# Last loads of a decode kernel reordered, value products placed by their landing, and a transposed FFN

## The chip, the cores and the metric

The kernel runs on one core of one Trainium2 chip. The metric is the device time of one execution in microseconds (us), the median of several runs. In the text, PE is TensorE (PEld its weight loads), DVE is VectorE, ACT is ScalarE, POOL is GpSimd and SP is SyncE, which here does nothing but issue transfers.

## What is computed

One decode step of a transformer layer in which attention and FFN work in parallel, for a batch of 4 with one token each:

```
xn = layernorm(x)                                  # x: 4 x 640
q  = xn @ wq                                       # 32 heads of 192
k, v = the last 2048 of 8192 cached positions      # per batch entry and head: 2048 x 192
o  = softmax(q k^T / sqrt(192)) v                  # per head
y  = x + o @ wo + (silu(xn @ w1) * (xn @ w3)) @ w2 # wo: 6144 x 640; w1, w3: 640 x 1536; w2: 1536 x 640
```

All inputs are bfloat16. The caches' windows are 32 key tiles and 32 value tiles of 3,072 KB; wq is 7,680 KB, wo is 7,680 KB, and w1, w3 and w2 are 1,920 KB each. Each byte is read once.

## The kernel before

**Tiles.** A head's keys are one tile `kt` of 128 partitions by 64 positions by 192: partition p holds 64 positions of one batch entry (32 partitions for each of the four entries). Its values are a tile `vt` of the same shape. There are two buffers for keys and three for values. The kernel writes its order by hand: `add(slot, phase, function, ...)` puts a step into a list, and the lists are run through by slot, and by phase within a slot. A slot u is a quarter of a head (16 positions); head h has the slots 4h to 4h+3, and 128 slots (`NU`) cover 32 heads. Every engine takes its instructions in that order.

**Scores.** `mult` (L202, DVE) multiplies a quarter of the key tile with the head's query, broadcast over the partitions. `adder` (L213, PE) adds six groups of 32 channels by six matmuls with the identity into a PSUM bank (two of these). `reduce_quarter` (L221, DVE) sums the 32 that are left. In slot u stand the product of u, the matmuls of u-1 and the reduction of u-2.

**Softmax.** For each head, over six slots: maximum in each partition (L225, DVE), transpose (L230, PE), maximum of each batch entry and its negative (L235, L238, DVE), broadcast back to the partitions (L243, PE), copy and exponential (L246, L249, ACT), and `chain_z` (L257, DVE), which spreads the exponentials over four columns, one for each batch entry. `ge_tot` (L278, PE) and `ge_norm` (L284, DVE) give the reciprocal of the sum.

**Values.** `pv` (L266, PE) is 32 matmuls for a head, each over two positions at once: 8 columns of z against 384 columns of V. The wanted results are two blocks of the product, the even position's in columns 0 to 191 and the odd position's in columns 192 to 383, on different partitions. `pv` comes in two halves of 16 matmuls, at slots 4h+10 and 4h+12 (`L` is 10). After the second, ACT copies the whole bank (128 x 384) to `o_raw` (L272). `ge_tr` (L294, PE) turns it and adds the blocks: six steps, each with one matmul for each of the two blocks, against the selection matrix `sel`; the profile counts 24 float32 matmuls for a head. `ge_copy` (L303, DVE) scales with the reciprocal into `oT`. For each group of four heads, `ge_proj` (`acc_add`, L194 and L195) multiplies with a tile of wo into two accumulators that live through the whole program; wo has two buffers.

**FFN.** w1, w3 and w2 share one buffer. `ffn_in` (L326) computes the gate and the up projection with xn as the weights: 15 matmuls of 512 columns for each matrix, copied by ACT; then SiLU (L331), the product (L337) and 12 transposes (L342). The product with w2 (24 matmuls of L194 and L195, behind everything else) ends the accumulation. L402 (DVE) and L403 (ACT) cast the accumulators, and L404 writes the output.

**Loads.** All transfers are issued by SP in program order, and SP waits where a buffer isn't free: x (L110), wq in three pieces (L116), the key tiles (L91, head h at slot 4(h-1)), the value tiles (L100, head h at slot 4h+2; head 29 at 4h+5; head 31 in two halves), wo (L106, group g at slot 16g+8, the last at slot 128), w1 and w3 (L318, slots 24 and 30), and w2 in three pieces (L350, slot 130). K31 is the key tile of head 31, V31 its value tile; wo6 and wo7 are the last two tiles of wo.

Of the kernel before, what the change touches and what calls it, by code (L numbers as in the profile page):

```python
# [10 lines left out]
FP32 = mybir.dt.float32  # L11
BF16 = mybir.dt.bfloat16
ALU = mybir.AluOpType
ACTF = mybir.ActivationFunctionType
AX = mybir.AxisListType
# [3 lines left out]
def kernel(  # L19
# [14 lines left out]
    KBUFS: int = 2,  # L34
    VBUFS: int = 3,
    PBUFS: int = 4,
    L: int = 10,
    FFN_HEAD: int = 6,
):
    nc = tc.nc  # L40
    P = 128
    B, Sq, D = A_x.shape
    _, H, Sk, Dh = A_k_cache.shape
    W = min(4096, max(256, Sk // 4))
    F = B_w1.shape[1]
    KC = D // P
    FC = F // P
    PB = P // B
    NJ = W // PB
    GQ = 4  # L50
# [4 lines left out]
    NG = H // HG  # L55
    CT = 32
    QW = HG * Dh
    RPP = QW // P
    NU = H * GQ
    N0 = D // 2  # L60
    N1 = D - N0
    QC = 512
# [1 line left out]
    assert D % P == 0 and F % QC == 0 and P % B == 0 and W % (PB * GQ) == 0  # L64
    assert JQ * DD == 512 and JQ % 2 == 0 and 2 * Dh <= 512 and 0 < N1 <= 512
    assert (H * Dh) % QC == 0 and NQ % 6 == 0 and QW % P == 0 and Dh % RPP == 0 and P == HG * CT
    assert 2 * H * Dh <= NJ * Dh and KBUFS == 2 and VBUFS == 3 and L == 10

    ctx.enter_context(tc.manual_schedule())
    const = ctx.enter_context(tc.tile_pool(name="const", bufs=1))  # L70
    fpool = ctx.enter_context(tc.tile_pool(name="ffn", bufs=1))
# [4 lines left out]
    small = ctx.enter_context(tc.tile_pool(name="small", bufs=3))  # L76
# [3 lines left out]
    ps_t = ctx.enter_context(tc.tile_pool(name="ps_t", bufs=1, space=MemoryType.PSUM))  # L80
# [3 lines left out]
    k_win = A_k_cache[:, :, Sk - W:Sk, :]  # L84
    v_win = A_v_cache[:, :, Sk - W:Sk, :]
    kts, vts, prs, pss, scs, exs, zs = {}, {}, {}, {}, {}, {}, {}
    wos, o_raws, rsums, rtbs, chs, ges, oTs = {}, {}, {}, {}, {}, {}, {}

    def load_k(h):
        kt = kpool.tile([P, NJ, Dh], BF16, tag="kt")  # L90
# [1 line left out]
                          in_=k_win[:, h].rearrange("b (p j) d -> p b (j d)", p=PB))  # L92
        kts[h] = kt

    def load_v(h, pieces=1):
        vt = vpool.tile([P, NJ, Dh], BF16, tag="vt")
        src = v_win[:, h].rearrange("b (p j) d -> p b j d", p=PB)
        n = NJ // pieces
        for i in range(pieces):
            nc.sync.dma_start(out=vt[:, i * n:(i + 1) * n, :].rearrange("q j d -> q (j d)"),  # L100
                              in_=src[:, :, i * n:(i + 1) * n, :].rearrange("p b j d -> p b (j d)"))
        vts[h] = vt

    def wo_load(hg):
# [2 lines left out]
        wos[hg] = wo_t  # L107

    x_sb = const.tile([B, D], BF16, name="x_sb")
    nc.sync.dma_start(out=x_sb[:], in_=A_x.rearrange("b s d -> (b s) d"))  # L110
    wq_v = A_wq.rearrange("(p kc) n -> p kc n", kc=KC)
    wq_rows = []
    for k0 in range(0, KC, 2):
        n = min(2, KC - k0)
        wt = vpool.tile([P, 2, H * Dh], BF16, tag="vt")
        nc.sync.dma_start(out=wt[:, 0:n, :].rearrange("p k n -> p (k n)"),  # L116
                          in_=wq_v[:, k0:k0 + n, :].rearrange("p k n -> p (k n)"))
        wq_rows += [wt[:, i, :] for i in range(n)]
    for h in range(KBUFS):
        load_k(h)  # L120

    idb = const.tile([P, P], BF16, name="idb")
    make_identity(nc, idb[:])
    idf = const.tile([P, P], FP32, name="idf")
# [6 lines left out]
    mask_b = const.tile([P, B], BF16, name="mask_b")  # L131
    nc.vector.tensor_copy(out=mask_b[:], in_=mask_f[:])

    sel = const.tile([P, 2 * B], FP32, name="sel")
    nc.vector.tensor_reduce(out=sel[:], in_=idf[:].rearrange("q (c k) -> q k c", k=CT)[:, 0:2 * B, :],
                            axis=AX.X, op=ALU.add)

    xf = ppool.tile([B, D], FP32, tag="pr")
    nc.vector.tensor_copy(out=xf[:], in_=x_sb[:])
# [22 lines left out]
    xnT = const.tile([P, KC, PB, B], BF16, name="xnT")  # L162
# [4 lines left out]
    for c0 in range(0, NQ, 6):  # L167
        qps = [pool.tile([P, QC], FP32, tag=tag, name="qps")
               for pool, tag in ((ps_add, "ps"), (ps_add, "ps"), (ps_o, "o_ps"), (ps_o, "o_ps"), (ps_m, "mt"), (ps_t, "t"))]
        for kc in range(KC):  # L170
            for i, qp in enumerate(qps):
                nc.tensor.matmul(qp[:], lhsT=xnT[:, kc].rearrange("p a b -> p (a b)"),  # L172
                                 rhs=wq_rows[kc][:, (c0 + i) * QC:(c0 + i + 1) * QC],
                                 start=(kc == 0), stop=(kc == KC - 1))
        for i, qp in enumerate(qps):
            dst = qbc[:, (c0 + i) * QC:(c0 + i + 1) * QC]
# [6 lines left out]
    o_banks = []  # L183
    for i in range(2):
        o_ps = ps_o.tile([P, 2 * Dh], FP32, tag="o_ps", name="o_ps")
# [7 lines left out]
    def acc_add(lhsT, rhs, first=False, last=False):  # L193
        nc.tensor.matmul(acc0[:], lhsT=lhsT, rhs=rhs[:, 0:N0], start=first, stop=last)  # L194
        nc.tensor.matmul(acc1[:], lhsT=lhsT, rhs=rhs[:, N0:D], start=first, stop=last)  # L195
# [62 lines left out]
                                in1=mask_b[:].unsqueeze(1).to_broadcast([P, NJ, B]), op=ALU.mult)  # L258
        zs[h] = z

    def pv(h, half):
        o_ps, z, vt = o_banks[h % 2], zs[h], vts[h]
        n = NJ // 4
        for jj in range(half * n, (half + 1) * n):
            c = jj % 4
            nc.tensor.matmul(o_ps[c * CT:c * CT + 2 * B, :], lhsT=z[:, 2 * jj:2 * jj + 2, :],  # L266
                             rhs=vt[:, 2 * jj:2 * jj + 2, :], start=(jj < 4), stop=(jj >= 2 * n - 4))
        if half == 1:
            zs.pop(h)
            vts.pop(h)  # L270
            o_raw = small.tile([P, 2, Dh], FP32, tag="o_raw", bufs=2, name="o_raw")
            nc.scalar.copy(out=o_raw[:].rearrange("q two d -> q (two d)"), in_=o_ps[:])  # L272
            o_raws[h] = o_raw


    def ge_tot(h):
# [10 lines left out]
    def ge_tr(h):  # L287
        hl = h % HG
        sl = slice(hl * CT, (hl + 1) * CT)
        gp = ps_t.tile([P, RPP, B], FP32, tag="t", name="gp")  # L290
        o_raw = o_raws.pop(h)
        for i in range(RPP):
            for part in range(2):
                nc.tensor.matmul(gp[sl, i, :], lhsT=o_raw[:, part, i:Dh:RPP], rhs=sel[:, part * B:(part + 1) * B],  # L294
                                 start=(part == 0), stop=(part == 1))
        ges[h] = gp

    def ge_copy(h):
# [9 lines left out]
        for i in range(i0, i1):  # L308
            acc_add(oT[:, i, :], wo_t[:, i * D:(i + 1) * D])

    h_sb = const.tile([B, F], BF16, name="h_sb")
    hT = const.tile([P, FC, B], BF16, name="hT")
    g_bf = const.tile([B, F], BF16, name="g_bf")
    ffn = {}

    def ffn_load(name, w):
# [1 line left out]
        nc.sync.dma_start(out=wt[:].rearrange("p k n -> p (k n)"), in_=w.rearrange("(p kc) n -> p (kc n)", kc=KC))  # L318
        ffn[name] = wt

    def ffn_in(name, dst):
        wt = ffn.pop(name)
        for n0 in range(0, F, QC):
            gt = ps_t.tile([B, QC], FP32, tag="t")
            for kc in range(KC):
                nc.tensor.matmul(gt[:], lhsT=xnT[:, kc, 0, :], rhs=wt[:, kc, n0:n0 + QC],  # L326
                                 start=(kc == 0), stop=(kc == KC - 1))
            nc.scalar.copy(out=dst[:, n0:n0 + QC], in_=gt[:])

    def ffn_silu():  # L330
        nc.scalar.activation(out=h_sb[:], in_=g_bf[:], func=ACTF.Silu)  # L331

    def ffn_up():
        ffn_in("w3", g_bf)

    def ffn_h():
        nc.vector.tensor_tensor(out=h_sb[:], in0=h_sb[:], in1=g_bf[:], op=ALU.mult)  # L337

    def ffn_transpose():
        hT_ps = ps_t.tile([P, FC, B], BF16, tag="t")  # L340
        for c in range(FC):
            nc.tensor.transpose(out=hT_ps[:, c, :], in_=h_sb[:, c:F:FC], identity=idb[0:B, 0:B])  # L342
        nc.vector.tensor_copy(out=hT[:], in_=hT_ps[:])

    w2_v = B_w2.rearrange("(p c) n -> p c n", c=FC)

    def w2_load(pieces):
        wt = fpool.tile([P, FC, D], BF16, tag="w", name="w2")
        for c0, c1 in pieces:
            nc.sync.dma_start(out=wt[:, c0:c1, :].rearrange("p c n -> p (c n)"),  # L350
                              in_=w2_v[:, c0:c1, :].rearrange("p c n -> p (c n)"))
        ffn["w2"] = wt

    sched = defaultdict(list)

    def add(slot, phase, fn, *args):
        sched[slot].append((phase, len(sched[slot]), fn, args))

    for h in range(H):
        u0, ul = h * GQ, h * GQ + GQ - 1  # L360
        if h >= KBUFS:
            add((h - KBUFS + 1) * GQ, 0, load_k, h)
        add(h * GQ + (2 if h != H - 3 else 5), 0, load_v, h, 1 if h < H - 1 else 2)
        for u in range(u0, ul + 1):
            add(u, 1, mult, u)
            add(u + 1, 2, adder, u)
            add(u + 2, 4, reduce_quarter, u)
        add(u0 + L, 3, pv, h, 0)
        add(u0 + L + 2, 3, pv, h, 1)
        add(ul + 2, 5, chain_lmax, h)  # L370
        add(ul + 3, 4, chain_tr, h)
        add(ul + 4, 5, chain_gmax, h)
        add(ul + 5, 4, chain_bc, h)
        add(ul + 6, 5, chain_z, h)
        add(ul + 6, 4, ge_tot, h)
        add(ul + 6, 6, ge_norm, h)
        add(u0 + L + 3, 3, ge_tr, h)
        add(u0 + L + 4, 5, ge_copy, h)
    for hg in range(NG):
        a = ((hg + 1) * HG - 1) * GQ + L + 5  # L380
        add(hg * HG * GQ + 8 if hg < NG - 1 else NU, 0, wo_load, hg)
        add(a, 3, ge_proj, hg, 0, RPP // 2)
        add(a + 1, 3, ge_proj, hg, RPP // 2, RPP)
    f = FFN_HEAD * GQ
    add(f, 0, ffn_load, "w1", B_w1)
    add(f + 5, 7, ffn_in, "w1", g_bf)
    add(f + 6, 7, ffn_silu)
    add(f + 6, 8, ffn_load, "w3", B_w3)
    add(f + 12, 7, ffn_up)
    add(f + 13, 7, ffn_h)  # L390
    add(f + 15, 7, ffn_transpose)
    add(NU + 2, 1, w2_load, [(0, FC // 2), (FC // 2, FC - 2), (FC - 2, FC)])

    for s in sorted(sched):
        for phase, _, fn, args in sorted(sched[s], key=lambda e: (e[0], e[1])):
            fn(*args)

    w2 = ffn.pop("w2")
    for c in range(FC):
        acc_add(hT[:, c, :], w2[:, c, :], last=(c == FC - 1))  # L400
    res = ppool.tile([B, D], BF16, tag="pr", name="res")
    nc.vector.tensor_copy(out=res[:, 0:N0], in_=acc0[:])  # L402
    nc.scalar.copy(out=res[:, N0:D], in_=acc1[:])  # L403
# [31 lines left out]
```

## Time and profile before

| What | Value |
|---|---|
| median of 5 runs | 534.62 us (532.68 to 535.16) |
| the profiled execution, time | 534.91 us |
| the profiled execution, span on the core | 533.1 us |
| mean clock granted to PE in it | 0.862 |
| PE busy | 380.3 us (71%) |
| DVE busy | 349.5 us (66%) |
| ACT busy | 48.1 us (9%) |
| read from HBM | 222.96 MB, 418 GB/s over the span |

The span is what the profiler's records cover on the core; the execution's time is 1.8 us longer. A group's row gives the source line, the engine, the operation with output and input, its shape and count, then busy time in all, mean ns of one, and the idle time of the engine just before these instructions with what ended most of it.

### The profile page before, as it was taken

What the parts mean: (1) busy time and instruction counts of PE and PEld (TensorE: products, weight loads), DVE (VectorE), ACT (ScalarE), POOL (GpSimd) and SP (SyncE); (2) the same over time, 40 slices, a digit from 0 to 9 for tenths busy, and PEclk for the clock granted to TensorE, in tenths of its full rate; (3) what the DMA queues carried; (4) which work ended last, traced back from release to release, by engine and by line L of the source; (5) the groups of instructions that cost most, each with busy time, mean ns of one, the idle gap of its engine ahead of it and who ended that gap; (6) DMA issues with size and microseconds to landing.
All of it is one profiled execution on the core that took longest, in us unless ns stands there. A gap on an engine that the chain in (4) does not pass through costs nothing.

```text
span 533.1 us, 6724 instructions
## 1 busy us (share of the span) xinstructions
PE 380.3 (71%) x2949; PEld 175.3 (33%) x2949; DVE 349.5 (66%) x471; ACT 48.1 (9%) x150; POOL 1.1 (0%) x8
## 2 busy tenths in 40 slices
PE   1876675759676686676848888566948777576987
PEld 0322232324232343233413334233413333232445
DVE  3178675867464776786756777587757776487861
ACT  2111100000222000000000000000000000000011
POOL 0000000000000000000000000000000000000000
PEclk9889877978789999597986779798897897798799
DMA  8999999999999999999999999999999999999993
GB/s 349 426 433 433 414 436 435 438 420 438 427 435 436 422 433 426 443 425 430 435 432 429 435 427 434 433 430 433 428 436 424 435 426 440 425 435 382 418 403 123
DMA packets 11709, 223.39 MB, mean 419 GB/s; under 512 B 1304, under 2 KB 1312, under 8 KB 2720
## 3 DMA queue, kind: packets, MB, share of 16 engines
q1 hardware_dynamic: 11680, 222.97, 97.8%
q8 instruction: 23, 0.38, 0.3%
q14 instruction: 6, 0.05, 0.0%
HBM read 222.96 MB, written 0.01 MB: 418 GB/s over the span
## 4 chain that ended last, share of the span: by engine, by line
DMA 59%; DVE 22%; PE 18%; issue 1%; ACT 0%; SPq 0%
DMA kt<-in_A_k_cache_dram 55%; DVE pr L202 16%; PE ps L213 8%; PE gp L294 5%; DVE sc L221 4%; DMA wt<-in_A_wq_dram 3%; PE qps L172 2%; PE o_ps L266 1%; PE acc L194 1%; PE acc L195 1%; DVE oT L303 0%; DVE rtb L284 0%; DVE qbc L178 0%; ACT o_raw L272 0%; DVE o_ps L186 0%
## 5 line engine op out<-in xcount | busy, mean ns | idle before, releaser
L213 PE MATMUL ps<-pr,idb 128*128 128x512 bf16 x768 | 222.7, 435 | 129.5 <-DVE sc L221 126.2
L202 DVE TENSOR_TENSOR pr<-kt,qbc 128x3072 bf16<-128x3072 bf16 x128 | 223.9, 1751 | 104.7 <-DMA kt<-in_A_k_cache_dram 103.6
L213 PEld LDWEIGHTS <-idb 128*128 128x128 bf16 x768 | 78.3, 106 | 226.1 <-issue 170.7
L221 DVE TENSOR_REDUCE sc<-ps 128x16 f32<-128x512 f32 x128 | 87.7, 685 | 8.2 <-PE ps L213 7.3
L266 PE MATMUL o_ps<-vt,z 128*8 128x384 bf16 x1024 | 58.1, 350 | 0.0
L294 PEld LDWEIGHTS gp<-sel,o_raw 128*32 128x32 f32 x768 | 46.8, 151 | 20.4 <-issue 18.7
L272 ACT COPY o_raw<-o_ps 128x384 f32<-128x384 f32 x32 | 15.3, 478 | 410.3 <-PE o_ps L266 410.3
L294 PE MATMUL gp<-sel,o_raw 128*32 128x4 f32 x768 | 49.6, 199 | 1.1 <-ACT o_raw L272 0.6
L266 PEld LDWEIGHTS <-z 128*8 128x8 bf16 x1024 | 20.9, 88 | 40.7 <-issue 29.9
L284 DVE RECIPROCAL rtb<-mt 32x4 f32<-32x4 f32 x32 | 5.7, 178 | 30.5 <-PE gp L294 30.5
L172 PE MATMUL qps<-wt,xnT 128*128 128x512 bf16 x60 | 17.0, 450 | 5.9 <-DMA wt<-in_A_wq_dram 5.9
L178 DVE CAST qbc<-qps 128x512 bf16<-128x512 f32 x6 | 3.8, 685 | 19.7 <-PE qps L172 19.7
L257 DVE TENSOR_TENSOR z<-ex,mask_b 128x256 bf16<-128x256 bf16 x32 | 13.3, 417 | 2.8 <-ACT ex L249 2.8
L194 PE MATMUL acc<-wo_t,oT 128*4 128x320 bf16 x48 | 13.4, 299 | 0.3 <-DVE oT L303 0.3
L195 PE MATMUL acc<-wo_t,oT 128*4 128x320 bf16 x48 | 13.4, 299 | 0.0
L326 PE MATMUL gt<-w,xnT 128*4 128x512 bf16 x30 | 9.3, 452 | 5.5 <-DVE oT L303 2.9
L243 PEld LDWEIGHTS mt<-ones_ff,gneg 1*128 1x128 f32 x64 | 9.4, 182 | 10.2 <-issue 9.9
L243 PE MATMUL mt<-ones_ff,gneg 1*128 1x1 f32 x64 | 12.1, 256 | 0.0
L172 PEld LDWEIGHTS <-xnT 128*128 128x128 bf16 x60 | 6.7, 112 | 15.8 <-issue 10.6
L249 ACT ACTIVATE ex<-sc,negm 128x64 bf16<-128x64 f32 x32 | 11.1, 348 | 1.0
L230 PE MATMUL mt<-idf,lmax 128*1 128x128 f32 x32 | 9.2, 286 | 0.0
L235 DVE TENSOR_REDUCE gmax<-mt 1x4 f32<-1x128 f32 x32 | 8.6, 269 | 0.7 <-PE mt L230 0.7
(58 smaller groups left out, 92.0 us busy)
## 6 DMA issues: line engine op xcount, KB each, us to landing
kt<-in_A_k_cache_dram SPq DMA_DIRECT2D x32, 3072.0 KB, 21.2
vt<-in_A_v_cache_dram SPq DMA_DIRECT2D x31, 3072.0 KB, 25.3
wo_t<-in_A_wo_dram SPq DMA_DIRECT2D x8, 960.0 KB, 20.7
wt<-in_A_wq_dram SPq DMA_DIRECT2D x2, 3072.0 KB, 10.1
w<-in_B_w_dram SPq DMA_DIRECT2D x2, 1920.0 KB, 25.0
vt<-in_A_v_cache_dram SPq DMA_DIRECT2D x2, 1536.0 KB, 12.5
wt<-in_A_wq_dram SPq DMA_DIRECT2D x1, 1536.0 KB, 20.1
w<-in_B_w_dram SPq DMA_DIRECT2D x1, 960.0 KB, 17.3
```

The costliest lines, as they stand in the source:

```text
L172: nc.tensor.matmul(qp[:], lhsT=xnT[:, kc].rearrange("p a b -> p (a b)"), rhs=wq_rows[kc][:, (c0 + i) * QC:(c0 + i + 1) * QC], start=(kc == ...
L194: nc.tensor.matmul(acc0[:], lhsT=lhsT, rhs=rhs[:, 0:N0], start=first, stop=last)
L195: nc.tensor.matmul(acc1[:], lhsT=lhsT, rhs=rhs[:, N0:D], start=first, stop=last)
L202: nc.vector.tensor_tensor(out=pr[:], in0=kts[h][:, g * JQ:(g + 1) * JQ, :], in1=qbc[:, h * Dh:(h + 1) * Dh].unsqueeze(1).to_broadcast([P, ...
L213: nc.tensor.matmul(ps[:], lhsT=idb[:], rhs=pr[:, :, kk * DD:(kk + 1) * DD], start=(kk == 0), stop=(kk == NK - 1))
L221: nc.vector.tensor_reduce(out=scs[h][:, g * JQ:(g + 1) * JQ], in_=pss.pop(u)[:], axis=AX.X, op=ALU.add)
L243: nc.tensor.matmul(mt[:, P:P + 1], lhsT=gneg[:].rearrange("o p b -> o (p b)"), rhs=ones_ff[0:1, 0:1], start=True, stop=True)
L249: nc.scalar.activation(out=ex[:], in_=scs.pop(h)[:], func=ACTF.Exp, bias=negm[:, 0:1], scale=SCALE, accum_out=rsum[:])
L257: nc.vector.tensor_tensor(out=z[:], in0=ex[:].unsqueeze(2).to_broadcast([P, NJ, B]), in1=mask_b[:].unsqueeze(1).to_broadcast([P, NJ, B]), ...
L266: nc.tensor.matmul(o_ps[c * CT:c * CT + 2 * B, :], lhsT=z[:, 2 * jj:2 * jj + 2, :], rhs=vt[:, 2 * jj:2 * jj + 2, :], start=(jj < 4), stop= ...
L272: nc.scalar.copy(out=o_raw[:].rearrange("q two d -> q (two d)"), in_=o_ps[:])
L294: nc.tensor.matmul(gp[sl, i, :], lhsT=o_raw[:, part, i:Dh:RPP], rhs=sel[:, part * B:(part + 1) * B], start=(part == 0), stop=(part == 1))
```

## The change

The change touches the end of the load order, the place of the value products, the merging of their two blocks, the FFN and the depth of the score pipeline. Line numbers of the changed kernel are up to 20 higher.

- **Loads.** x is issued by ACT. V29, V30 and V31 (in pieces of 48 and 16 positions), the first four of w2's twelve rows, wo6, wo7, and the rest of w2 in pieces of 3, 3 and 2 rows are issued in this order at slot 122, behind K31 (slot 120). w3 is issued at slot 32, behind K9.
- **Score pipeline.** The reduction of u stands in slot u+1, no longer u+2, and the softmax steps stand one to two slots sooner.
- **Value products.** `L` is 8: a head's 32 matmuls stand in one block at slot 4h+8. For the last three heads a table (`ends`) gives the slots: 126, 130, and 133 with 134 (24 and 8 matmuls). The projections of wo6 and wo7 stand at slot 136, with w2's first piece ahead of them and its other pieces behind.
- **Merge.** ACT writes the odd block, scaled by a 0/1 column, to `o_odd` (128 x 192), and a new DVE instruction (`pv_merge`) adds the masked even block from PSUM; `ge_tr` then has one matmul, not two, in each of its six steps.
- **FFN.** Gate and up are computed transposed: for each of 12 chunks of 128 outputs, five matmuls with a chunk of the matrix as the weights (its columns taken at a step of 12) and 4 columns of xn. SiLU and the product work on 128 x 48, and the transposes go.

The core of the diff:

```diff
-    nc.sync.dma_start(out=x_sb[:], in_=A_x.rearrange("b s d -> (b s) d"))
+    nc.scalar.dma_start(out=x_sb[:], in_=A_x.rearrange("b s d -> (b s) d"))
...
-            o_raw = small.tile([P, 2, Dh], FP32, tag="o_raw", bufs=2, name="o_raw")
-            nc.scalar.copy(out=o_raw[:].rearrange("q two d -> q (two d)"), in_=o_ps[:])
+        nc.scalar.activation(out=o_odd[:], in_=o_ps[:, Dh:2 * Dh], func=ACTF.Copy, scale=half[:, 1:2])
...
+    def pv_merge(h):
+        o_raw = small.tile([P, Dh], FP32, tag="o_raw", bufs=2, name="o_raw")
+        nc.vector.scalar_tensor_tensor(out=o_raw[:], in0=o_banks[h % 2][:, 0:Dh], scalar=half[:, 0:1],
+                                       in1=o_odds.pop(h)[:], op0=ALU.mult, op1=ALU.add)
...
-            for part in range(2):
-                nc.tensor.matmul(gp[sl, i, :], lhsT=o_raw[:, part, i:Dh:RPP], rhs=sel[:, part * B:(part + 1) * B],
-                                 start=(part == 0), stop=(part == 1))
+            nc.tensor.matmul(gp[sl, i, :], lhsT=o_raw[:, i:Dh:RPP], rhs=sel[:], start=True, stop=True)
...
+        for c in range(c0, c1):
             for kc in range(KC):
-                nc.tensor.matmul(gt[:], lhsT=xnT[:, kc, 0, :], rhs=wt[:, kc, n0:n0 + QC],
+                nc.tensor.matmul(ffn["ps"][:, c, :], lhsT=ffn[name][:, kc, c:F:FC], rhs=xnT[:, kc, 0, :],
                                  start=(kc == 0), stop=(kc == KC - 1))
-            nc.scalar.copy(out=dst[:, n0:n0 + QC], in_=gt[:])
...
+    W2C = [0, FC // 3, FC // 3 + 3, FC - 2, FC]
...
+    VCUT = NJ * 3 // 4
+    ends = {H - 3: (NU - 2, NU + 3), H - 2: (NU + 2, NU + 4), H - 1: (NU + 6, NU + 7)}
...
-            add(u + 2, 4, reduce_quarter, u)
-        add(u0 + L, 3, pv, h, 0)
-        add(u0 + L + 2, 3, pv, h, 1)
-        add(ul + 2, 5, chain_lmax, h)
-        add(ul + 3, 4, chain_tr, h)
-        add(ul + 4, 5, chain_gmax, h)
-        add(ul + 5, 4, chain_bc, h)
-        add(ul + 6, 5, chain_z, h)
+            add(u + 1, 8, reduce_quarter, u)
+        add(ul + 1, 9, chain_lmax, h)
+        add(ul + 2, 3, chain_tr, h)
+        add(ul + 2, 4, chain_gmax, h)
+        add(ul + 3, 3, chain_bc, h)
+        add(ul + 3, 4, chain_z, h)
...
+        v, m = ends.get(h, (u0 + L, u0 + L + 1))
+        if h < H - 1:
+            add(v, 7, pv, h)
+        else:
+            add(v - 1, 7, pv, h, 0, VCUT)
+            add(v, 7, pv, h, VCUT, NJ)
+        add(m, 0, pv_merge, h)
+        add(m, 7, ge_tr, h)
+        add(m + 1, 0, ge_copy, h)
...
+    for h in range(H - 3, H - 1):
+        add(NU - 6, 0, load_v, h)
+    add(NU - 6, 0, load_v, H - 1, (0, VCUT, NJ))
+    add(NU - 6, 0, w2_load, 0)
+    add(NU - 6, 0, wo_load, NG - 2)
+    add(NU - 6, 0, wo_load, NG - 1)
+    for i in range(1, 4):
+        add(NU - 6, 0, w2_load, i)
+    add(e - 2, 8, ffn_out, 0)
+    for hg in range(NG - 2, NG):
+        add(e, 6, ge_proj, hg, 0, RPP)
+    for i in range(1, 4):
+        add(e, 7, ffn_out, i)
```

## The prediction

> **What bounds the kernel now.** I read the page's slices first, then the chain of waits, then the DMA view and the timeline of the last 45 us. The slices and the queue:
>
> ```profile
> DMA  8999999999999999999999999999999999999993
> GB/s 349 426 433 433 414 436 435 438 420 438 427 435 436 422 433 426 443 425 430 435 432 429 435 427 434 433 430 433 428 436 424 435 426 440 425 435 382 418 403 123
> q1 hardware_dynamic: 11680, 222.97, 97.8%
> ```
>
> The DMA engines are full from the second slice to the 39th. Only the last slice is empty: the transfers end before the program does. The engines that compute are not full:
>
> ```profile
> L213 PE MATMUL ps<-pr,idb 128*128 128x512 bf16 x768 | 222.7, 435 | 129.5 <-DVE sc L221 126.2
> L202 DVE TENSOR_TENSOR pr<-kt,qbc 128x3072 bf16<-128x3072 bf16 x128 | 223.9, 1751 | 104.7 <-DMA kt<-in_A_k_cache_dram 103.6
> ```
>
> DVE waits 103.6 us for key tiles, 3.6 us in each of 29 waits. So until the last key tile the run goes at the pace of the bytes, and what an engine gains there is lost in the wait for the next tile. What is left is the end. The DMA view (last figure: us from issue to landing) and the timeline:
>
> ```profile
> w<-in_B_w_dram SPq DMA_DIRECT2D x1, 960.0 KB, 17.3
> w<-in_B_w_dram SPq DMA_DIRECT2D x1, 320.0 KB, 18.7
> ```
>
> ```profile
> 529.98 0.30 PE L195 MATMUL acc<-w,hT 128*4 128x320 bf16 x1
> 530.18 0.48 DVE L402 CAST res<-acc 4x320 bf16<-4x320 f32 x1 [5.01 <-PE acc L194]
> 530.32 0.41 ACT L403 CAST res<-acc 4x320 bf16<-4x320 f32 x1 [6.97 <-PE acc L195]
> 530.76 0.30 SPq L404 DMA_DIRECT2D out_dram<-res  x1
> ```
>
> The w2 pieces are issued at 506.2 to 507.1, so they land from 523.5 to 525.8 (507.1 + 18.7). The last matmul starts at 529.98 and the span ends at 533.1: 3.1 us of casts and output that no order can hide, and 4.2 us between the last byte and the last matmul. Those 4.2 us are the value products and projections of the last heads, which follow K30's landing at 488.84:
>
> ```profile
> 488.84 1.76 DVE pr L202
> ...
> 522.87 0.49 ACT o_raw L272
> 523.40 1.56 PE gp L294 x24
> 524.99 0.20 DVE oT L303
> 525.23 0.30 PE acc L194
> ```
>
> This is the chain in order of time (start, us, engine, line); the lines left out are DVE and PE too, and no transfer stands in it after 488.84. Two paths therefore run side by side after K30, the transfers and this chain; the end is the later one plus 3.1.
>
> **Part by part: the transfers.** The order of bytes changes, not their number. x leaves SP's queue: wq is issued at 0.73 in place of 1.16, so everything lands 0.4 earlier. wo6 (960 KB, 2.3 us at the 433 GB/s of full slices) moves behind V31: K30 and K31 land 2.3 + 0.4 earlier, 486.1 and 493.4 (now 488.84, and 484.5 + 11.6 = 496.1). V29 and V30 wait for products that are over by then; V31, now issued at 504.3 behind the product of head 28, goes out with K31: the product of head 28 that frees its buffer now stands in the slot in which K31 is issued. In the kernel before (here and below "now") its two pieces land at 515.2 and 518.9, 8.3 us after V30 (510.6), where one tile takes 7.25 (K31 after K30): 1.0 us too long, at 350 GB/s in 510 to 514 with the engines 0.98 busy. Busy engines mean slow packets, not an empty queue; the pieces remain pieces, so nothing here says that it goes. Bounds 0 and -1.0; I take -0.5. The w2 pieces get smaller; the last 960 KB now (640 and 320) land in 525.8 - 523.5 = 2.3 us, full rate, so 0. Last landing: 525.8 - 0.4 - 0.5 = 524.9. Behind it stand two rows of w2, four matmuls 0.136 apart: 0.1 + 0.4 + 3.1 gives a span of 528.5 by this path.
>
> On the short pieces the Trainium skill (DMA: Bandwidth & Descriptors, Bandwidth) speaks against the change: transfers should be at least 1 MiB, and its fit gives each a fixed 2.0 us. Two more such pieces would by that be an estimated +4 us; the 2.3 us above show no such cost between queued pieces.
>
> **The chain after K30.** From the row durations, DVE without stalls: head 30 is 4 products of 1.76, 4 reductions of 0.61, maximum 0.25, two steps of gmax 0.5, z 0.45, reciprocal and oT 0.4, and the new merge. The merge has no row: between a 64-column reduction (0.21) and a 512-column one (0.69); I take 0.35, nearer the first by columns. That is 11.4; head 31 without merge and oT 10.85. Then the last reduction waits for its six matmuls (1.46 after the product): 1.4; maximum, transpose, gmax, broadcast, exponential and z, from rows of 0.2 to 0.5 each: 3.0. So z of head 31 ends 26.7 after K30 (now 488.84 to 520.89: 32.0, with the steps spread over two slots more). PE meanwhile finishes the broadcast at 25.4, then: product of head 30 (32 matmuls, twice the 0.82 of 16) to 27.05; sums and transposition of 29 to 28.0 (24 matmuls took 1.56, the merged form has 12: 0.75); merge and transposition of 30 to 29.4; product of 31 to 31.05; first w2 piece 8 x 0.136 to 32.15; transposition of 31 to 32.95; two projections, 24 x 0.136, to 36.2; 15 more starts to 38.3. From 486.1: last matmul 524.4, span 527.5. That is the lower end.
>
> Stalls are the upper end. The timeline:
>
> ```profile
> 491.25 2.72 PE L213 MATMUL ps<-pr,idb 128*128 128x512 bf16 x6 [3.52 <-DVE sc L221]
> 505.30 1.47 PE L213 MATMUL ps<-pr,idb 128*128 128x512 bf16 x6
> ```
>
> The reduction then comes one slot after its product, not two, so DVE waits for six matmuls: 1.46 at full clock, inside the next product's 1.76, but 2.72 at half clock, 1.1 more; behind that wait stand DVE's next product and the K load that this product releases. The windows show a mean clock of 0.57 from 488 to 500, so two or three slots pay: +2.6, span 530.1. The middle is 528.8; against 528.5 of the transfers, the later of the two is likeliest some 0.3 above either: **529.0**. Around the span of the profiled execution lie 534.91 - 533.1 = 1.8 us: **530.8**. The median of the five runs, 534.62, is 0.3 below that execution; I leave this in the range.
>
> **What is hidden, and by what.** In the run before K30 each head adds the merge (0.35) and loses half of ACT's copy and 0.75 of PE: cover is the 3.6 us wait for the key tile. The merge waits for ACT's half and stands ahead of a product; its value product runs while DVE waits for the key tile, so ACT (9% busy) is through by then. The product of a head comes two slots sooner, but its V stands in the queue ahead of the K that opens that slot, so it has landed. K2 at the start is issued about 1 us later (the first reduction waits for matmuls at half clock); V0 lands at 27.1 + 16.9 = 44.0, so the queue is not empty then. The FFN's 30 matmuls of 512 columns (9.3) and copies become 120 loads and matmuls with 4 columns, with weights at a step of 12. Nearest are the 12 transposes of L342 with that step: 0.9 together, 75 ns each, so 4.5 for each matrix. If nothing overlapped, 159 + 195 ns each, 21 per matrix. I take 4.5: those 12 are the same form. PE and DVE stand still for it; the cover is the queue. A key tile takes 21.2 us to land (median) and 7.25 of that are its own: 14 us of other transfers are queued. When the first matrix held PE, and so DVE for 6.75 us before 145.17, the DMA share of the windows from 134 to 150 stayed between 0.93 and 1.10.
>
> **Rivals.**
> *The tail on PE at half clock.* Matmuls after the broadcast of head 31 are 8.7 us at full clock. If waits for V30 and V31 leave PE idle, they take up to twice that; but PE returned to full clock after 8.6 us of work (491.25 to 499.87), so at most half of it, +4.3. For it: PE idle 3.52 us before 491.25, then clock 0.5. Against it: the chain keeps PE packed from the broadcast on. Time 530.8 + 1.0 to 4.3, typically 532.6. Chance 0.2.
> The Trainium skill (TensorE: Matmul & The Clock Gate, Part 1) has the half clock come after an idle window of about 3.4 us and go after one as long of sustained work; by that the cost would be an estimated 1.7 us, not 4.3.
> *K31 issued too late.* It waits for the last product of K29, now 10.1 us after K29 landed (474.34, 484.46); the stalls make that 11 to 12.7, and K30 ends 14.5 after K29. Already the engines fall to a share of 0.75 in 484 to 488, though K31 still lands 7.25 after K30. Beyond about 13 the slowest engine idles too: +0.5 to 2. Time about 532.0. Chance 0.12.
> *Starvation in the middle; slower.* If DVE's stalls exceed 3.6 us in a head, the run no longer goes at the pace of the bytes. Three cold slots of 1.1 plus merge are 3.65: the limit is in reach, though the mean clock of 0.862 says that only about a quarter of the time is cold. From there every 0.2 us in each of 29 heads costs 5.8 us; with the FFN at 21 us each, 3.4 us for each matrix beyond the 17.6 of cover. Time 537 to 541. Chance 0.06.
> *The transfers were never late* (the change does not do what it says: wo6 and w2 last only move the wait). Then the chain decides alone: 38.3 to 40.9 after K30 (now 41.1), time 529.3 to 531.9, mostly inside the forecast and counted there.
>
> **How the numbers follow.** Forecast 0.62, the half clock 0.2, K31 0.12, starvation 0.06. Lower end: transfers with the whole 1.0 (span 528.0), chain without stalls: 529.8 in time, 529.2 with the median's 0.3 and some for the fetches of instructions, which share the queue's engines. Upper end: 533.8, into the half-clock case; starvation and the worst of half clock stay out. About 0.3% (1.6 us) is what a measurement can tell: under 533.0 is faster. Forecast, half of the half clock and most of K31 lie there: 0.81; same 0.13; slower 0.06 from starvation.
>
> **What would show it.** Right: the last slice fuller; K31 landing near 493.4; the last w2 piece at 524 to 525.5 and the last matmul within 1 us of it; the waits of DVE for key tiles still there, 2 to 3 us in each head. Wrong: the last matmuls back to back long after the landing with clock 0.5 (half clock); a gap in the DMA share before K31; waits of DVE for matmuls over 100 us in total (starvation).

## The result, and the profile after

| | before | changed |
|---|---|---|
| median of all runs | 533.72 us (54 runs, 532.58 to 535.17) | 531.79 us (29 runs, 530.01 to 534.74) |
| the profiled execution: time, span | 534.91, 533.1 us | 531.72, 529.9 us |
| mean clock granted to PE | 0.862 | 0.903 |

The ratio is 0.9963, 95% interval 0.9955 to 0.9972: faster by 0.37%. The forecast was 530.8 us, 1.0 below the median, which lies inside its range. The gain is 1.9 us, half of what was forecast (534.62 to 530.8 is 3.8): 1.0 of the difference is the changed kernel, and 0.9 is the kernel before, whose median fell from 534.62 in five runs to 533.72 in 54.

The slices and the queue of the changed kernel, from the page:

```profile
DMA  8999999999999999999999999999999999999995
GB/s 358 438 423 413 428 442 421 439 423 427 438 430 434 430 428 435 429 432 429 430 440 428 434 420 441 428 434 428 434 435 427 437 425 434 430 436 380 442 380 222
q1 hardware_dynamic: 11816, 222.96, 98.4%
```

The bytes are the same; the last slice is fuller (222 GB/s, was 123): less time passes behind the last byte. The engines that compute, from the groups of the page:

```profile
L216 PE MATMUL ps<-pr,idb 128*128 128x512 bf16 x768 | 214.5, 421 | 160.1 <-DVE pr L205 160.1
L205 DVE TENSOR_TENSOR pr<-kt,qbc 128x3072 bf16<-128x3072 bf16 x128 | 224.0, 1750 | 108.7 <-DMA kt<-in_A_k_cache_dram 108.4
...
L224 DVE TENSOR_REDUCE sc<-ps 128x16 f32<-128x512 f32 x128 | 87.4, 682 | 2.6 <-PE ps L216 1.5
```

DVE still waits 108.4 us for key tiles, and only 1.5 us for score matmuls. So up to the last key tile the bytes set the pace, as before. Now the end, as the chain of waits has it in order of time (start, us, what):

```profile
486.43 33.23 DMA wo_t<-in_A_wo_dram
519.66 0.04 issue
519.70 0.30 PE acc L197
520.00 0.20 PE acc L198
520.19 0.27 PE acc L197
...
523.39 0.18 PE acc L197
523.57 0.14 PE acc L198
...
526.83 0.15 PE acc L198
```

The chain that ended last now runs back to a transfer, wo6, which landed at 519.66. Behind it stand 40 matmuls, at first 0.27 us apart and later 0.14. The windows show why (after the busy times of the engines: granted clock, DMA share, GB/s):

```profile
508.00:512.00 4.00, 2.84 (x35) 1.34 (x37) 1.61 (x6) 0.60 (x3) 0.00 (x0) 0.71 0.88 318
...
516.00:520.00 4.00, 2.09 (x31) 1.37 (x24) 0.60 (x2) 0.42 (x1) 0.00 (x0) 0.99 1.01 426
520.00:524.00 4.00, 4.00 (x19) 2.03 (x18) 0.00 (x0) 0.00 (x0) 0.00 (x0) 0.58 0.88 357
524.00:528.00 4.00, 2.97 (x22) 1.66 (x20) 0.48 (x1) 0.41 (x1) 0.00 (x0) 1.00 0.04 16
```

PE was half idle from 516 to 520, and from 519.9 to 523.4 it ran at half clock: mean 0.58 in the third line. The timeline of PE names the idle times (in brackets, with what ended them):

```profile
515.89 0.50 PE L268 MATMUL o_ps<-vt,z 128*8 128x384 bf16 x8 [0.17 <-DMA vt<-in_A_v_cache_dram]
517.41 0.30 PE L197 MATMUL acc<-w,hT 128*4 128x320 bf16 x1 [1.03 <-DMA w<-in_B_w_dram]
...
519.70 0.30 PE L197 MATMUL acc<-wo_t,oT 128*4 128x320 bf16 x1 [0.88 <-DMA wo_t<-in_A_wo_dram]
```

PE waits three times for a load that has not come: here the compute follows the transfers, where in the kernel before no transfer stood in the chain after 488.84. The other end of that path is the last step of the softmax, z of head 31, which came 10 us sooner (timelines of the kernel before and of the changed one):

```profile
520.46 0.43 DVE L257 TENSOR_TENSOR z<-ex,mask_b 128x256 bf16<-128x256 bf16 x1 [1.29 <-ACT ex L249]
```

```profile
510.51 0.42 DVE L260 TENSOR_TENSOR z<-ex,mask_b 128x256 bf16<-128x256 bf16 x1 [1.13 <-ACT ex L252]
```

For the experiments one table of such points says most. All are us from the start of the span, in the one profiled execution of each kernel: when DVE starts on K30, when z of head 31 is ready, when the last w2 piece has landed, when the last matmul starts, and how long after the landing that is ("lag"). From the last matmul to the end of the span it is 3.1 to 3.2 us in all of them.

| kernel | K30 | z of 31 | last landing | last matmul | lag | median (ratio to before, interval) |
|---|---|---|---|---|---|---|
| before | 488.8 | 520.9 | 525.8 | 530.0 | 4.2 | 533.72 |
| changed | 485.4 | 510.9 | 525.0 | 526.7 | 1.7 | 531.79 (0.9963, 0.9955 to 0.9972) |
| a1_old_loads | 487.2 | 512.8 | 525.9 | 528.0 | 2.1 | 533.01 (0.9990, 0.9966 to 1.0013) |
| a5_old_depth | 484.8 | 514.8 | 525.1 | 525.6 | 0.5 | 530.95 (0.9953, 0.9934 to 0.9972) |
| a4_fill | 486.2 | 511.8 | 526.4 | 527.0 | 0.6 | 531.43 (0.9959, 0.9943 to 0.9975) |
| a2_old_ffn | 487.4 | 513.5 | 527.2 | 527.7 | 0.5 | 533.28 (0.9997, 0.9984 to 1.0010) |
| c1_ffn_only | 490.3 | 519.8 | 528.4 | 531.0 | 2.7 | 535.73 (1.0050, 1.0032 to 1.0068) |
| b1_v31_whole | 484.8 | 510.4 | 523.7 | 524.3 | 0.6 | 529.54 (0.9936, 0.9912 to 0.9959) |
| c4_no_wo7 | 487.2 | 512.7 | 524.6 | 526.9 | 2.3 | 531.44 (0.9953, 0.9935 to 0.9971) |
| c3_a1_fill | 487.2 | 512.8 | 525.9 | 526.8 | 0.9 | 530.88 (0.9952, 0.9936 to 0.9967) |
| e1_a2_pad | 487.5 | 513.1 | 528.4 | 529.0 | 0.6 | 533.50 (1.0005, 0.9992 to 1.0017) |
| e3_c1_pad | 487.7 | 518.9 | 524.5 | 528.0 | 3.5 | 533.69 (1.0004, 0.9990 to 1.0017) |
| a3_old_merge | 485.0 | 510.5 | 527.1 | 527.8 | 0.7 | 531.85 (0.9972, 0.9952 to 0.9991) |
| d1_a5_whole | 485.5 | 516.9 | 524.2 | 526.3 | 2.1 | 530.47 (0.9944, 0.9928 to 0.9960) |

A single profiled execution says how the steps hang together; how fast a kernel is says its median. Executions differ in their start: DVE reaches head 1 at 41.4 us in the changed kernel's trace and at 43.3 in c4's, though their programs do not differ there, and K30 comes 443.9 and 443.8 later. The profiled execution of before was 1.2 us above its median, so the two traces lie 3.3 us apart where the medians lie 1.9 apart.

### The profile page after: what moved, and what is told of

Same layout as the page of the kernel before. It is cut to its first block, busy times and chain, and to the rows that moved or that the text cites. A ratio compares the mean times of both kernels' runs of the same rounds, so it can differ in the third digit from the quotient of the medians.

```text
span 529.9 us, 6169 instructions
## 1 busy us (share of the span) xinstructions
PE 349.1 (66%) x2643; PEld 165.3 (31%) x2643; DVE 362.7 (68%) x504; ACT 43.9 (8%) x144; POOL 1.1 (0%) x8
## 4 chain that ended last, share of the span: by engine, by line
DMA 62%; DVE 20%; PE 15%; ACT 1%; issue 1%; SPq 0%
DMA kt<-in_A_k_cache_dram 53%; DVE pr L205 14%; PE ps L216 8%; DMA wo_t<-in_A_wo_dram 6%; DVE sc L224 4%; DMA wt<-in_A_wq_dram 3%; PE qps L175 2%; PE gp L302 1%; DVE z L260 1%; ACT ex L252 1%; PE acc L197 1%; PE acc L198 1%; PE mt L246 1%; PE mt L233 0%; DVE qbc L181 0%
## 5 line engine op out<-in xcount | busy, mean ns | idle before, releaser
L216 PE MATMUL ps<-pr,idb 128*128 128x512 bf16 x768 | 214.5, 421 | 160.1 <-DVE pr L205 160.1
L205 DVE TENSOR_TENSOR pr<-kt,qbc 128x3072 bf16<-128x3072 bf16 x128 | 224.0, 1750 | 108.7 <-DMA kt<-in_A_k_cache_dram 108.4
L268 PE MATMUL o_ps<-vt,z 128*8 128x384 bf16 x1024 | 53.2, 342 | 0.2 <-DMA vt<-in_A_v_cache_dram 0.2
L268 PEld LDWEIGHTS <-z 128*8 128x8 bf16 x1024 | 24.3, 88 | 26.8 <-issue 15.0
L302 PEld LDWEIGHTS gp<-sel,o_raw 128*32 128x32 f32 x384 | 24.7, 151 | 16.4 <-issue 12.5
L275 ACT ACTIVATE o_odd<-o_ps,half 128x192 f32<-128x192 f32 x32 | 13.5, 420 | 185.6 <-PE o_ps L268 183.6
L302 PE MATMUL gp<-sel,o_raw 128*32 128x4 f32 x384 | 27.3, 200 | 0.8 <-DVE o_raw L280 0.8
L249 ACT COPY negm<-mt 128x1 f32<-128x1 f32 x32 | 5.1, 159 | 257.9 <-PE mt L246 257.9
L280 DVE SCALAR_TENSOR_TENSOR o_raw<-o_ps,half,o_odd 128x192 f32<-128x192 f32 x32 | 13.1, 410 | 3.3 <-ACT o_odd L275 3.3
L197 PE MATMUL acc<-wo_t,oT 128*4 128x320 bf16 x48 | 14.7, 321 | 0.9 <-DMA wo_t<-in_A_wo_dram 0.9
L198 PE MATMUL acc<-wo_t,oT 128*4 128x320 bf16 x48 | 14.7, 321 | 0.0
L233 PE MATMUL mt<-idf,lmax 128*1 128x128 f32 x32 | 11.4, 355 | 1.1 <-DVE lmax L228 1.1
```

The costliest lines, as they stand in the source:

```text
L205: nc.vector.tensor_tensor(out=pr[:], in0=kts[h][:, g * JQ:(g + 1) * JQ, :], in1=qbc[:, h * Dh:(h + 1) * Dh].unsqueeze(1).to_broadcast([P, ...
L216: nc.tensor.matmul(ps[:], lhsT=idb[:], rhs=pr[:, :, kk * DD:(kk + 1) * DD], start=(kk == 0), stop=(kk == NK - 1))
L275: nc.scalar.activation(out=o_odd[:], in_=o_ps[:, Dh:2 * Dh], func=ACTF.Copy, scale=half[:, 1:2])
L302: nc.tensor.matmul(gp[sl, i, :], lhsT=o_raw[:, i:Dh:RPP], rhs=sel[:], start=True, stop=True)
```

## The experiments

Four theories went into the first four runs. **A**: the shorter chain behind the last key tile is what gained. **B**: the order of the last loads is. **C**: the last byte sets the end, and PE's clock only fills a wait. **D**: the transposed FFN gains or loses by itself.

**a1_old_loads**: the load order of before in the changed kernel.

```diff
-    for h in range(H - 3, H - 1):
-        add(NU - 6, 0, load_v, h)
-    add(NU - 6, 0, load_v, H - 1, (0, VCUT, NJ))
...
+    add(NU - 7, 0, load_v, H - 3)
+    add(NU - 6, 0, load_v, H - 2)
+    add(NU - 2, 0, load_v, H - 1, (0, VCUT, NJ))
+    add(NU, 0, wo_load, NG - 1)
+    for i in range(4):
+        add(NU + 2, 1, w2_load, i)
```

> The changed kernel with the load order of before: wo6 early, V29 to V31 behind K31, then wo7 and w2 in four pieces; the projection of wo6 back in its old place, and w2's first piece behind the projection of wo7. Pipeline, merge and FFN stay changed. Theory A (the shorter chain behind the last key tile is what brought the end nearer to the last byte, and the order of the last loads is worth little): K30 lands 2.3 us later than in the changed kernel, about 487.6, but 1.6 us of projection leave the tail; the last matmul is bound by the last piece of w2 at about 525.0 to 525.5; span 528.8 to 529.8, ratio to before 0.994 to 0.997. Rival B (the order of the last loads is what gained): the kernel falls back to the time of before, ratio 0.999 to 1.001.

Measured 533.01 us, ratio 0.9990 with an interval of a quarter per cent to each side: rather B than A, but not decided by itself.

**a5_old_depth**: the score pipeline, softmax steps and `L` of before, with the new loads. A head's value product stays one block, now at slot 4h+10, and the FFN stands two slots sooner.

```diff
-            add(u + 1, 8, reduce_quarter, u)
-        add(ul + 1, 9, chain_lmax, h)
...
+            add(u + 2, 4, reduce_quarter, u)
+        add(ul + 2, 5, chain_lmax, h)
...
```

> The changed kernel with the score pipeline and the softmax steps of before (reduction two slots after its product, z six slots after the last product, L of 10); the loads, the merge, the FFN and the slots of the last heads stay changed. Theory A: z of head 31 again ends about 32 us after K30 has landed (485.3), at 517.3 in place of 510.9; 12 us of PE work follow, so the last matmul starts at about 529.3; span 532 to 533, ratio to before 1.000 to 1.003. Rival B (the order of the last loads is what gained): the ratio stays at 0.995 to 0.998.

Measured 530.95 us, ratio 0.9953 (0.9934 to 0.9972). The chain is longer by 4.4 us (z of head 31 comes 30.0 after K30, not 25.6) and nothing is lost. The timeline of this kernel, DVE alone (the last line is the cast that follows the last matmul, L402 in the kernel before):

```profile
514.33 0.42 DVE L260 TENSOR_TENSOR z<-ex,mask_b 128x256 bf16<-128x256 bf16 x1
...
525.83 0.48 DVE L425 CAST res<-acc 4x320 bf16<-4x320 f32 x1 [5.80 <-PE acc L197]
```

z is there 10.3 us before the last landing (525.1), and what is left from z on takes some 9 (9.4 in d1 below, where PE waits for no load). Theory A in its plain form falls.

**a4_fill**: 20 unread matmuls of 128x512 in PE's waits of the tail.

```diff
+    for s_, ph, n_ in [(128, 4, 4), (129, 3, 2), (131, 8, 3), (132, 8, 4), (134, 7, 4), (135, 8, 3)]:
+        add(s_, ph, warm, n_)
```

> The changed kernel with 20 matmuls added that nobody reads (128 x 512, a constant against a constant, into a free PSUM bank), in the waits of PE behind the last six matmuls of scores. Theory A (the tail is late because PE is at half clock from 519.9 to 523.4): the clock stays at 1.0 to the end, the last matmul starts 0.5 us after the last piece of w2 has landed (525.0), span 528.3 to 529.0, ratio to before 0.993 to 0.995. Rival C (the last bytes set the end and the clock only fills the wait): no change against the changed kernel, ratio 0.996 to 0.998.

The clock stayed at full speed to the end and the lag fell from 1.7 to 0.6 us. The median, 531.43, is not told apart from the changed kernel's; in the profiled run the last byte came 1.4 later. So the half clock's cost is read from the trace (1.1 us) and not shown in the time.

**a2_old_ffn**: the FFN of before (`ffn_in` with xn as the weights, ACT's copies, the transposes) in the changed kernel.

> The changed kernel with the FFN of before (15 matmuls of 512 columns for each matrix, copies, 12 transposes), the rest as changed. Theory A (all of the FFN is hidden behind the queue of transfers in the middle): no difference, ratio to before 0.995 to 0.998, the wait of DVE for key tiles within 6 us of the changed kernel's 108.4. Rival D (the transposed FFN is what gained or lost): the ratio moves by 0.002 or more either way.

Measured 533.28 us: the gain is gone. The table says that the lag is small (0.5) and that the bytes came late: K30 2.0 and the last landing 2.1 after the changed kernel's. Either the FFN itself costs this (D), or something else in that build does. The opposite edit should tell.

**c1_ffn_only**: the kernel before, with the transposed FFN alone.

> The kernel before with one part of the change: the transposed FFN (its 120 loads and matmuls, at slots 31 and 39 of its schedule in place of 29, 36 and 39); loads, depth, merge and tail as before. Theory D (the transposed FFN itself spares the transfers some 1.8 us, which is why the changed kernel with the FFN of before lost its gain): about 531.9, ratio 0.9965. Theory E (the FFN is hidden behind the queue in either form; where the loss came from lies outside it, in when the bytes of that build come): 533.5, ratio 0.9985 to 1.0015.

Measured 535.73 us, slower than before by 0.5%: neither theory. D has the wrong sign here, and E allowed 0.15%. The durations of the single 24 KB packets (128 of them make a key or value tile) between 60 and 450 us of the span gave the answer; ns, and beside it where the key tiles begin in SBUF, as the remainder of the address in each partition by 256:

```
                 address   mean    10%   median   90%
before                 0   913.7   912    912     912
changed                0   913.9   912    912     912
a2_old_ffn            64   917.3   913    914     921
c1_ffn_only          192   917.5   913    914     921
```

The packets of both losing kernels are 0.4% longer, and over some 445 us of full queue 0.4% is 1.8 us. Both edits change the constant tiles' size, and so where all later tiles lie. Theory F: it is the address.

**e1_a2_pad** and **e3_c1_pad**: one unused constant tile of 64 bytes per partition added to a2 and to c1.

```diff
+    const.tile([P, 32], BF16, name="pad")
     idb = const.tile([P, P], BF16, name="idb")
```

> The changed kernel with the FFN of before (533.3 us) and one unused constant tile of 64 bytes per partition, which moves the key and value tiles from addresses that leave 64 when divided by 128 to multiples of 128; no instruction differs. Theory F (the address alone: at an odd multiple of 64 the 24 KB packets take 917 ns in the mean, else 913.5, and over 450 us of full queue that is the loss of 1.5 to 2 us; the FFN is hidden in either form): packets back at 912 to 914, 531.8, ratio 0.9965. Theory D (the form of the FFN): packets and time as without the tile, 533.3, ratio 0.9997.

> The kernel before with only the transposed FFN (535.7 us, its tiles at an odd multiple of 64 too) and the same unused tile of 64 bytes, which moves them to multiples of 256; no instruction differs. Theory F: packets back at 912 to 914 and the time of before, 533.3, ratio 0.9985 to 1.0015. Theory D: 535.7, ratio 1.005.

e3: 533.69 us, ratio 1.0004, where c1 without the tile had 535.73 and 1.0050; the packets are back at 912 (mean 913.8). The DMA view of both from 60 to 450 us (packets, MB, share of the engines' time; a packet counts whole where it begins), first c1, then e3:

```profile
q1 hardware_dynamic: 8438, 166.90, 100.1%
```

```profile
q1 hardware_dynamic: 8479, 167.76, 100.2%
```

Both queues are full, yet c1 moves 0.5% fewer bytes. No instruction differs: here the address is shown to be the cause, and the transposed FFN by itself to be worth nothing (0.9990 to 1.0017). e1 did not recover: 533.50 us. Its tiles went from 64 to 128 past a multiple of 256, and its packets stayed at 917.0. So the limit of 128 that the expectation named is wrong; 256 fits all 14 traces (mean packets, 11 at multiples of 256: 913.3 to 913.9; three others: 917.0 to 917.5), though that limit was drawn after the fact, from e1. The old FFN in the changed kernel at a multiple of 256 was not tried, so that a2 and e1 lost by the address alone is argued from c1 and e3.

The Trainium skill (DMA: Bandwidth & Descriptors, How a descriptor splits into AXI transactions) says that a transaction that reads must begin at a multiple of 256 bytes and that a descriptor that begins elsewhere costs extra beats. The limit agrees, but what moved here is the address that is written, and by that account 64, 128 and 192 would cost different amounts, where the three runs cost the same.

**b1_v31_whole**: V31 as one transfer in the changed kernel.

```diff
-    add(NU - 6, 0, load_v, H - 1, (0, VCUT, NJ))
+    add(NU - 6, 0, load_v, H - 1)
```

> The changed kernel with V31 loaded as one transfer of 3072 KB in place of 2304 and 768. If the cut makes the first piece slow (6.44 us for 2304 KB, where full rate gives 5.44), the tile takes 7.3 us, the last w2 piece lands 1.0 sooner and the time is 530.8, ratio 0.9945. If the slow stretch is not the cut's (slow packets, instruction fetches on the same engines), the tile takes 8.3 to 8.6 as now, and the time is that of the changed kernel, 531.8, ratio 0.9963.

Measured 529.54 us, ratio 0.9936 (0.9912 to 0.9959): the cut costs. V31 lands 7.27 us after V30, where cut it took 8.57; d1 below repeats it, 7.27 where a5 has 8.33. The last landing comes 1.3 sooner, 0.8 sooner counted from K30. Another 1.0 us that this trace gains is lag, for its half clock fell earlier (515.7 to 519.1); whether the edit moved it is not shown. The cut makes packets of 18 KB that took 769 ns in the mean, where 684 would be the rate of the 24 KB ones; uncut, all of V31's took 912. The timeline of PE, b1:

```profile
514.49 1.62 PE L268 MATMUL o_ps<-vt,z 128*8 128x384 bf16 x32 [1.22 <-DMA vt<-in_A_v_cache_dram]
...
520.65 0.30 PE L197 MATMUL acc<-wo_t,oT 128*4 128x320 bf16 x1 [0.18 <-DMA wo_t<-in_A_wo_dram]
```

All 32 matmuls now wait for the whole tile, which the cut was to spare, and it costs nothing: they are over 0.1 us after w2's first piece has landed (515.97). This version has the lowest median here.

**c4_no_wo7**: no load of wo7; the last projection reads wo6's tile.

```diff
-    add(NU - 6, 0, wo_load, NG - 1)
...
-        oT, wo_t = oTs[hg], wos[hg]
+        oT, wo_t = oTs[hg], wos[min(hg, NG - 2)]
```

> The changed kernel without the load of wo7 (960 KB); the last projection reads wo6's tile instead, so the output is not the reference's, and PE's work is unchanged. If the last bytes set the end (theory C), everything behind comes 2.2 to 2.3 us sooner: 529.5, ratio 0.992. If PE's work in the tail at half clock also sets it, only a part comes: 530.3 to 531, ratio 0.9935 to 0.995. If the chain behind the last key tile alone set the end (theory A), nothing: 531.8, ratio 0.9963.

Measured 531.44 us; A fits best by the median, but the trace shows what happened. From K30 to the last landing it is 37.5 us, 2.2 less than in the changed kernel, as C has it. But wo6 lands at 521.54, and the 40 matmuls behind it, 0.136 apart, take 5.3 us at full clock: the last starts at 526.87, 2.3 after the last landing. So PE's work behind wo6 is a path of its own. In the changed kernel three such paths end almost together, counted at full clock up to the start of the last matmul: from wo6 (519.7) with 40 matmuls 525.0, from wo7 (521.96) with 28 matmuls 525.7, from the last w2 piece (525.02) with four 525.5. The measured 526.7 is 1.0 above the latest, which is the price of the half clock once more. The path from wo7 then sets the end wherever the clock is full and z early: in a4 wo7 lands at 523.29, in a5 at 521.92 and in b1 at 520.61, and 28 matmuls from there give 527.0, 525.6 and 524.3, as measured; so it is in a2, e1 and a3. Their lag of 0.5 to 0.7 is this path, not the four matmuls behind the last piece.

The trace of c4 also started 1.8 us later; whether its eight runs did so (529.15 to 532.67) can't be seen.

**c3_a1_fill**: a1 with the 20 matmuls of a4.

> The load order of before in the changed kernel (as in the first of these runs, 533.0 us) with the 20 unread matmuls of 128x512 in PE's waits of the tail. If the old order lost only because PE's work behind the last landing ran at half clock (its last matmul started 2.1 us after the landing), it now starts about 0.5 after: 531.4, ratio 0.9958. If it lost because its bytes come later, or because more work stands behind the last landing than the clock explains, the time stays at 532.5 to 533.0, ratio 0.998 to 0.999.

Measured 530.88 us (0.9936 to 0.9967), where a1 had 533.01. The last byte lands at the same 525.9 in both traces; the lag is 0.9 in place of 2.1 (1.2 of the 2.1 us between the medians), and the clock stays full in the tail. What a1's trace lost is the half clock from 517.8 to 524.6; the other 0.9 between the medians no trace shows, and a1's 12 runs spread from 530.0 to 536.6. With PE kept busy the two load orders are not told apart (530.88 here, 531.43 in a4). So B falls too in its plain form: in these traces the old order loses only with the half clock.

**a3_old_merge**: the merge of before in the changed kernel (ACT copies the whole bank, 24 matmuls).

> The changed kernel with the merge of before: ACT copies the whole bank, no merge on DVE, and 24 instead of 12 matmuls transpose each head. If the merge is hidden (before the last key tile by the wait for bytes, behind it by the wait for the last pieces), the time is that of the changed kernel, 531.8, ratio 0.996 to 0.997. If PE's tail is what sets the end, its 0.75 us more for each of the heads 30 and 31 come on top: 532.5 to 533.3, ratio 0.998 to 0.9995.

Measured 531.85 us, 0.9972: the merge is hidden, within an interval of 0.2%. Its trace shows something else. At half clock from 471.2 to 481.4, K31 was issued 12.9 us after DVE began on K29 (10.8 in the changed kernel), the DMA engines fell to a share of 0.49 from 480 to 484, and K31 landed 8.6 us after K30, not 7.4 (8.4 in a4 and 8.7 in c3, which ran at half clock shortly before as well). So the loss that the prediction's rival of a late K31 names does occur, about 1 us, in executions whose clock falls there.

**d1_a5_whole**: a5 with V31 as one transfer.

> Attempt at a better version: the changed kernel with the score pipeline, softmax steps and value products of before's depth (530.95 us) and V31 as one transfer (529.54 us with the new depth). Theory C (the last landing plus some 0.5 to 1 plus 3.2): the landing is that of the whole V31, the last matmul within 1 us of it: 529.0 to 529.6, ratio 0.992 to 0.9935. If the longer chain of the old depth, z of head 31 at 514 to 515, decides as soon as the bytes come 1.3 sooner: 530.3 to 531, ratio 0.9945 to 0.9955.

Measured 530.47 us, the second theory. The timeline of DVE, d1:

```profile
516.44 0.42 DVE L260 TENSOR_TENSOR z<-ex,mask_b 128x256 bf16<-128x256 bf16 x1
...
526.48 0.48 DVE L425 CAST res<-acc 4x320 bf16<-4x320 f32 x1 [5.13 <-PE acc L197]
```

z of head 31 ends at 516.9 and the last matmul starts 9.4 later, 2.1 after the last landing. With the old depth the chain is back on the path as soon as the bytes come 1.3 sooner; a half clock from 517.7 to 521.1 is part of its 9.4 us. The new depth, which alone gains nothing, has z some 4 us sooner (510.9 in the changed kernel, 514.8 in a5), and b1's trace has room for that. The medians of d1 and b1, 530.47 and 529.54, are not told apart by their intervals.

## Why the prediction was right, and where its steps were not

- **Two paths, and the later one sets the end: right.** Of the 3.3 us that the span of the trace lost, 0.8 are the earlier landing and 2.5 the lag (4.2 to 1.7).
- **Last landing 524.9: measured 525.0, by two errors that cancel.** The x on ACT gave its 0.4 (wq issued at 0.73, and K0 landed at 29.04, not 29.51). K30 was used from 485.4, not 486.1; why it came 0.7 sooner is open. V31 failed: I took half of a possible gain of 1.0, and it took 8.57 us behind V30, 0.2 more than before. b1 shows that the cut is the cause, worth 1.3 us of transfer; the medians lie 2.2 apart, with intervals that overlap a little (0.9936, 0.9912 to 0.9959, against 0.9963, 0.9955 to 0.9972). The shorter pieces cost nothing, as the sum has it: two of 480 KB landed in 2.28 us behind wo7 and 320 KB in 0.78 more. The fixed 2.0 us that the prediction takes from the Trainium skill is a fit for transfers issued from GpSimd (DMA: Bandwidth & Descriptors, Anatomy of one DMA); these are issued by SP.
- **Chain after K30: right in DVE's part, 25.6 us to z (26.7).** The stalls of up to 2.6 did not come: DVE waited 1.5 us for score matmuls in the whole run. That was luck in part, for no half clock fell between 475.6 and 509.7. PE's part did not run back to back from z on, as I had summed it: it waits for w2's first piece and wo6, and the sum has to begin at wo6's landing. The step that failed is the last matmul "within 1 us" of the landing; it came 1.7 after. The sum counted 0.5 for the four matmuls behind the last piece, but 28 stand behind wo7 (0.7 after the landing at full clock), and the half clock adds 1.0.
- **The half clock in the tail: came, as the rival with 0.2 had it, at its lower end.** Its price in the trace is 1.1 us (lag 1.7 against 0.6 in a4), and that is what separates the forecast span of 529.0 from 529.9. The argument against it failed: the chain did not keep PE packed. PE worked 1.6 of the 3.4 us before 519.9, waiting for w2 and wo6 in stretches of at most 1.03, and the clock fell. The rival's 8.7 us of matmuls are too few as well: the prediction's own list behind the broadcast, 25.4 to 38.3, is 12.9 long. I had the half clock go after 8.6 us of work; here the two stretches in the tail, 509.7 to 513.1 and 519.9 to 523.4, last 3.4 us each; other runs show 6.8. The Trainium skill (TensorE: Matmul & The Clock Gate, Part 1) gives 3.4 us of sustained work, which these two stretches bear out and the longer ones do not; the idle window that it sets ahead of a half clock did not come before 519.9.
- **K31 issued too late: not here.** From K29 to K31's issue it was 10.8 us (470.88 to 481.64), and K31 landed at 492.8 (493.4). The margin is thin: the share of the DMA engines fell to 0.77 from 480 to 484, and in the traces of a4, c3 and a3 K31 landed 0.9 to 1.3 us later behind K30.
- **Starvation: no.** DVE's waits for key tiles grew to 3.9 us in a head where I had 2 to 3.
- **FFN hidden: right,** and 4.5 us for each matrix was near: 60 loads (160 ns) and matmuls (198 ns) overlap and hold PE for 3.6 (173.7 to 177.3 for w3). The danger was one that the prediction did not have: c1, where the same edit leaves the tiles off a multiple of 256 bytes, loses 0.4%. The changed kernel moved them by 5,888, a multiple of 256, which was luck.
- **What gained.** Not one part: z of head 31 has to come early enough before the last landing. Where z is late (before, e3, d1), 9.1 to 9.4 us pass from z to the last matmul, and the end follows z: z stands 4.9, 5.6 and 7.3 us before the last landing there, and in c1 8.6. In all others it is 10.3 or more, and the end follows the loads and the clock. The new loads bring K30 sooner against the last landing (40.3 us before it in a5, 37.0 in before), the new depth brings z sooner behind K30 (25.6 us, 32.0 in before). Either was enough, the loads alone by a narrow margin: z comes 30.0 us behind K30 in a5. a5 (new loads, old depth) and c3 (old loads, new depth, PE kept busy) both keep the whole gain, 530.95 and 530.88. With neither, e3 has a lag of 3.5 and the time of before. Both runs keep the new place of the value products, which was not undone by itself: what it adds stays open.

## What to carry to other kernels

Where bytes set the pace, look for the paths behind the last key tile one by one, each from the landing that starts it: shortening one, or reordering the loads, gains only down to the next, and here three of them end within a microsecond. Before a whole-program difference of half a per cent is put down to an edit, compare the durations of equal packets and the tiles' addresses: an unused tile of 64 bytes was worth as much as the change. Cutting a transfer had a price here (1.3 us), and the wait for the whole tile had none: compare the two before cutting.

## What the runs showed of the hardware

- A 24 KB packet into SBUF took 912 ns (median) where its tile begins at a multiple of 256 bytes, else 914 to 915 and a mean 0.4% higher, with remainders of 64, 128 and 192 alike.
- Packets of 18 KB out of rows of 24 KB took 769 ns in the mean in the changed kernel, 12% more than their bytes at the rate of whole rows; the last quarter, 6 KB, took 237, near the 228 by bytes. In all nine kernels with this cut it is 769 to 819 and 234 to 238.
- Stretches of half clock in the 14 traces last 3.4 us or a multiple of it (6.8, 10.2, 13.7, once 20.5), and where one falls decides what it costs: in b1 it lay from 515.7 to 519.1, ahead of the last loads, and the lag stayed at 0.6; in a1 from 517.8 to 524.6, and the lag was 2.1.
